# Attention with stride masks, a rotating token mixer and a gated mixture of attention experts: q loaded as diagonal blocks, float64 weights rebuilt in three bit operations and in halves, masks of 128 rows, the values of a pair in a row

## The chip, the cores and the metric

The kernel runs on one core of a Trainium2 chip. The metric is the device time in microseconds, as the median of several runs. The core has a matrix engine (TensorE; PE in the profile, PEld for its weight loads), VectorE (DVE), ScalarE (ACT), GpSimd (POOL) and SyncE (SP), which here only issues transfers.

## The reference

Four batches of 576 positions go through three blocks. The first is attention over 8 heads of 64; the first four heads see a window of 32 positions, the last four see positions that are equal modulo 32. The second mixes tokens and channels. The third is a mixture of four attention experts with a gate.

```python
# block 1, per head: local or strided mask, both causal
scores = scale * q @ k.T                     # scale = 1/8
scores = where(mask, scores, -1e9)
attn   = exp(scores - max); attn /= sum + 1e-9
x      = attn @ v                            # joined heads: (4, 576, 512)
# block 2
theta  = x @ w_theta                         # 512 x 512
y      = w_tok_r @ (x * cos(theta)) + w_tok_i @ (x * sin(theta))   # 576 x 576 each
u      = x + y
x      = u + max(u @ w_ch, 0)                # 512 x 512
# block 3: per expert q, k, v, causal attention, wo; the best two by gate are summed
```

The weights of block 2 arrive as float64.

## The kernel before

Everything is held with channels on the partitions: `X[b]` is batch b as 4 chunks of 128 channels by 576 positions. A float32 product at good precision is made of three matmuls (`mm3`, lines 240 to 243): each operand is split into a high and a low part, and high*high, high*low and low*high are added up.

**Block 1** is `attn_pair(b, pair)`, one call for each pair of heads: pairs 0 and 1 are local, 2 and 3 strided, and each pair has three groups of three or four tiles. For a group, q of two heads (288 KB a pair; k has 304 or 288 KB, v 432 or 297) is copied into a block-diagonal tile `qdiag` with the scale (lines 169 to 172: GpSimd for batch 0, ScalarE after), so that one matmul scores both heads. A mask matmul (line 178: bfloat16, 64 rows of `mask_l` or `mask_s` against `twice`, two identities side by side) opens the sum in PSUM, the score matmuls (line 182, float32, one for each tile) add to it. The softmax follows in one of two forms (`per_tile`, lines 193 to 203): either ScalarE takes the exponential of each tile with its maximum as bias, or VectorE subtracts the maximum and ScalarE takes all tiles at once. GpSimd divides (line 206), PE turns the probabilities (line 209), ScalarE moves them to SBUF (line 212), and PE multiplies by v (line 218: 64 output columns, two heads side by side in `av`); the result is copied into `X[b]` (lines 223 and 226). Each group does this by itself.

**The float64 weights** come through `load64` (lines 121 to 136), one chunk of 128 rows at a time, staged in `X[3]` and `X[2]`. ScalarE takes the magnitude of the upper word (131). VectorE then clamps it (132), shifts and masks it (133), ors in the top bits of the lower word (134) and the sign with the top exponent bit (135). `split_w` makes the high part on ScalarE and the low part on GpSimd or VectorE. `wth` (w_theta) has 4 chunks of 512, `wtk` (both token matrices) 9 chunks of 576, `wch` 4 chunks of 512.

**Block 2** for batch b is `theta(b, h)` and `rotate(b, h)` for the halves h = 0, 1 of the channels, then `tokens(b, h)`; `channels(b)` runs one batch later. `theta` has five tiles of positions of 12 matmuls each, in two PSUM buffers; VectorE reduces each result to one turn (264, 265), ScalarE takes the magnitude (266) and later cosine and sine (271, 272). `rotate` turns X on PE (279), multiplies on VectorE (289), and splits on ScalarE or VectorE (299, 301) and GpSimd (302). `tokens` is two halves of the positions by two chunks of 128 channels, 27 matmuls each.

**The order.** A planner (the tile framework) decides when each instruction goes out: each engine has one queue in program order of the planner's simulated schedule, and earlier code has priority when several are ready. The code's order is: pairs (0,0) and (0,1), `wth`, pairs (0,2) and (0,3); then for each batch theta, rotate, tokens, with the pairs of the next batch put between as filler. In batch 0 the whole of `wtk` is loaded right behind `theta(0, 0)`, line 369, and pairs (1,0) and (1,1) stand ahead of `tokens(0, 0)`. SP issues all transfers in one queue, and an issue that waits for a free buffer holds those behind it. `theta(b, 0)` needs all four pairs of its batch.

Of the kernel before, what the change touches and what calls it, by code (L numbers as in the profile page):

```python
# [32 lines left out]
MASKED = -1.0e9  # L33
INV2PI = 1.0 / (2.0 * math.pi)
# [3 lines left out]

TINY64 = float(np.array([0x38000000], np.uint32).view(np.float32)[0])
# [3 lines left out]
def fused_kernel(ctx: ExitStack, tc: tile.TileContext, ql, kl, vl, qs, ks, vs, wth, wtk, wch, wqk, wvg, wo, out):  # L43
    nc = tc.nc

    def f(ap):
        return ap.bitcast(F32)
# [10 lines left out]
    def select(ap, pattern, base, cm):  # L58
        nc.gpsimd.affine_select(out=ap, in_=ap, pattern=pattern, compare_op=ALU.is_ge, fill=MASKED,
                                base=base, channel_multiplier=cm)  # L60


    mask_l = new_mask("mask_l", [64, 4, LK])
    select(mask_l[:, 1, :], [[1, LK]], -1, -1)
    select(mask_l[:, 1, :], [[-1, LK]], WPAD, 1)
    nc.vector.tensor_copy(mask_l[:, 0, :], mask_l[:, 1, :])
    nc.vector.tensor_copy(mask_l[:, 2:4, :], mask_l[:, 1:2, :].to_broadcast([64, 2, LK]))
    nc.vector.memset(mask_l[:, 0, :WPAD], MASKED)
# [11 lines left out]
    mask_s = new_mask("mask_s", [64, 5, RQ])  # L80
    select(mask_s[:, 0, :], [[-1, RQ]], 0, 1)
    select(mask_s[:, 0, :], [[BLK, 3], [0, BLK]], BLK - 1, -1)
    nc.vector.tensor_copy(mask_s[:, 1:5, :], mask_s[:, 0:1, :].to_broadcast([64, 4, RQ]))
    nc.vector.memset(mask_s[:, 4, 2 * BLK:], MASKED)
    mask_c = new_mask("mask_c", [128, 128])
    select(mask_c, [[-1, 128]], 0, 1)
# [9 lines left out]
    qd = pha.enter_context(tc.tile_pool(name="qd", bufs=1, side="right"))  # L96
    qdiag = [[qd.tile([128, n, 2 * rw], F32, name=f"qdiag{rw}_{i}") for i in range(m)]
             for n, rw, m in ((3, LQ, 3), (4, RQ, 2))]
    for t in qdiag[0] + qdiag[1]:
        nc.vector.memset(t, 0.0)  # L100

# [19 lines left out]
    def load64(dst, src, kt, n, scale=1.0):  # L121


        hi, lo = dst
        for c in range(kt):
            raw = X[3].bitcast(U32).rearrange("p (a c) s -> p a (c s)", a=2)[:, c % 2, :2 * n]
            raw = raw.rearrange("p (n t) -> p n t", t=2)
            st = X[2][:, c % 4, :n]
            nc.sync.dma_start(raw, src[:, c, :].bitcast(U32).rearrange("p (n t) -> p n t", t=2))
# [6 lines left out]
            split_w(hi[:, c, :], lo[:, c, :], st, scale, nc.vector if c % 3 == 1 else nc.gpsimd)  # L136
# [5 lines left out]
    def attn_pair(b, pair, ps1, ain, apl, deep, qbufs, kbufs=2):  # L142
        local = pair < 2
        pj = pair % 2
        groups, rw, kw = (LOCAL, LQ, LK) if local else (STRIDED, RQ, RQ)
        kn = S + WPAD if local else S
        qr = ain.tile([128, S], F32, tag="q", bufs=qbufs, name=f"q_{b}_{pair}")
        kt = ain.tile([128, S + WPAD], F32, tag="k", bufs=kbufs, name=f"k_{b}_{pair}")
        nc.sync.dma_start(qr, (ql if local else qs)[b, pj])
        nc.sync.dma_start(kt[:, :kn], (kl if local else ks)[b, pj])  # L150
        loads = []
        for g, (j0, j1) in enumerate(groups):
            vg = ain.tile([128, 4, 2, HD], F32, tag="v", name=f"v_{b}_{pair}_{g}")
            nc.sync.dma_start(vg[:kw, :j1 - j0], (vl if local else vs)[b, pj, :, j0:j1])
            loads.append(vg)
        xo = X[b][:, pair, :]
        for g, (j0, j1) in enumerate(groups):
            vg = loads[g]
            n = j1 - j0

            qg = qdiag[pair // 2][(3 * pair + g) % len(qdiag[pair // 2])]
            q0, q1 = rw * j0, min(rw * j1, S)
            for h in range(2):
                hs = slice(64 * h, 64 * h + 64)
                for a, z_, m in ((q0, q1, n),) if (q1 - q0) % rw == 0 else ((q0, q0 + 2 * rw, 2), (q0 + 2 * rw, q1, 1)):
                    i0 = (a - q0) // rw
                    dst = qg[hs, i0:i0 + m, rw * h:rw * h + (z_ - a) // m]
                    src = qr[hs, a:z_].rearrange("p (n q) -> p n q", n=m)
# [39 lines left out]
            for i in range(n):  # L208
                nc.tensor.transpose(tp[:kw, i * rm:(i + 1) * rm], p[:rm, i * kw:(i + 1) * kw], ident[:rm, :rm])  # L209
# [3 lines left out]
            pt = pt[:, :n * rm].rearrange("p (n h q) -> p n h q", n=n, h=2)  # L213
            av = ps1.tile([128, 512], F32, tag="av", bufs=2, name=f"av_{b}_{pair}_{g}")
            for i in range(n):
                w = kw if local else wd[i]
                for h in range(2):
                    nc.tensor.matmul(av[64 * h:64 * h + 64, i * rw:i * rw + wd[i]], vg[:w, i, h, :],  # L218
                                     pt[:w, i, h, :wd[i]], start=True, stop=True)
            c = sum(wd)  # L220
            copy = nc.scalar.copy if b == 0 else nc.vector.tensor_copy
            if local:
                copy(xo[:, rw * j0:rw * j0 + c], av[:, :c])
            else:
                r0, nr = 3 * j0, c // BLK
                copy(xo.rearrange("p (t r) -> p r t", r=32)[:, r0:r0 + nr, :],
                     av[:, :c].rearrange("p (r t) -> p r t", t=BLK))
# [120 lines left out]
    with tc.tile_pool(name="ps0", bufs=2, space=PSUM) as ps0, tc.tile_pool(name="ain0", bufs=10) as ain0, \  # L348
            tc.tile_pool(name="apl0", bufs=6) as apl0:
        attn_pair(0, 0, ps0, ain0, apl0, 2, 4, 4)  # L350
        attn_pair(0, 1, ps0, ain0, apl0, 2, 4, 4)
        load64(wth_s, wth, 4, DM, INV2PI)
        for pair in range(2, 4):
            attn_pair(0, pair, ps0, ain0, apl0, 2, 4, 4)
# [7 lines left out]
    def next_pair(b, pair):  # L362
        if b + 1 < B:
            attn_pair(b + 1, pair, ps1, ain, apl, 1, 1)

    for b in range(B):
        theta(b, 0)
        if b == 0:
            load64(wtk_s, wtk, 9, S)
        else:  # L370
            next_pair(b, 0)
            channels(b - 1)
        rotate(b, 0)
# [19 lines left out]
        if b == 0:  # L393
            with tc.issue_after(sins[0, 1]):
                load64(wch_s, wch, 4, DM)
            next_pair(b, 2)
# [301 lines left out]
```

## Time and profile before

| | us |
|---|---|
| median of three runs | 602.59 |
| lowest, highest | 600.97, 603.19 |
| the profiled execution | 603.8 |
| its span on the core | 602.0 |
| PE busy | 571.9 (95%) |
| PE weight load busy | 525.3 (87%) |
| VectorE busy | 422.5 (70%) |
| ScalarE busy | 340.7 (57%) |
| GpSimd busy | 244.5 (41%) |

Matmuls are pipelined, so a PE that is busy all the time isn't one at its best pace: the step from one matmul's start to the next is the thing to read. The granted clock is a share of TensorE's 2.4 GHz. In the rows below, L182 is line 182 of the kernel; "x6" is the number of instructions in a row; what stands in square brackets is the idle time ahead of an instruction and what ended it.

### The profile page before, as it was taken

What the parts mean: (1) busy time and instruction counts of PE and PEld (TensorE: products, weight loads), DVE (VectorE), ACT (ScalarE), POOL (GpSimd) and SP (SyncE); (2) the same over time, 40 slices, a digit from 0 to 9 for tenths busy, and PEclk for the clock granted to TensorE, in tenths of its full rate; (3) what the DMA queues carried; (4) which work ended last, traced back from release to release, by engine and by line L of the source; (5) the groups of instructions that cost most, each with busy time, mean ns of one, the idle gap of its engine ahead of it and who ended that gap; (6) DMA issues with size and microseconds to landing.
All of it is one profiled execution on the core that took longest, in us unless ns stands there. A gap on an engine that the chain in (4) does not pass through costs nothing.

```text
span 602.0 us, 12582 instructions
## 1 busy us (share of the span) xinstructions
PE 571.9 (95%) x4560; PEld 525.3 (87%) x4560; DVE 422.5 (70%) x1209; ACT 340.7 (57%) x935; POOL 244.5 (41%) x336
## 2 busy tenths in 40 slices
PE   7985979899999999999999999999999999999997
PEld 5875859799999999989999999988989898989986
DVE  5689988794667646586545644289897878879881
ACT  4565796752655514646214532067577767857873
POOL 6763275441144411144300643345435624544452
PEclk9999878969999999999999999998999999999998
DMA  9723434121212111200010001100001000100112
GB/s 280 230 80 118 138 130 132 56 76 30 81 38 62 34 52 40 70 17 22 7 53 1 1 18 37 36 1 1 1 2 51 30 2 31 41 12 4 38 41 78
DMA packets 17365, 32.67 MB, mean 54 GB/s; under 512 B 2056, under 2 KB 9400, under 8 KB 17304
## 3 DMA queue, kind: packets, MB, share of 16 engines
q1 hardware_dynamic: 17304, 31.88, 17.3%
q8 instruction: 36, 0.59, 0.4%
q14 instruction: 25, 0.20, 0.1%
HBM read 27.15 MB, written 4.72 MB: 53 GB/s over the span
## 4 chain that ended last, share of the span: by engine, by line
PE 75%; DVE 12%; ACT 6%; issue 3%; DMA 2%; POOL 1%; POOLq 0%; DVEq 0%; ACTq 0%; SPq 0%
PE s L182 7%; PE y L241 6%; PE y L242 6%; PE y L243 6%; PE av L218 3%; PE tp L540 3%; PE tp L209 3%; PE g L241 3%; PE g L242 3%; PE g L243 3%; PE th L241 3%; PE th L242 2%; PE th L243 2%; PE o L564 2%; PE pq L241 2%
## 5 line engine op out<-in xcount | busy, mean ns | idle before, releaser
L241 PE MATMUL y<-wtk_hi,zhi 128*128 128x288 f32 x288 | 87.7, 305 | 0.4 <-DVE X L317 0.4
L242 PE MATMUL y<-wtk_lo,zhi 128*128 128x288 f32 x288 | 87.0, 302 | 0.0
L243 PE MATMUL y<-wtk_hi,zlo 128*128 128x288 f32 x288 | 86.2, 300 | 0.0
L302 POOL TENSOR_TENSOR zlo<-cs,zhi 128x512 fp32r<-128x512 f32 (+1 forms) x40 | 49.6, 1250 | 64.6 <-DVE zhi L299 40.2
L537 POOL TENSOR_SCALAR p<-p,sm,gt 128x256 f32<-128x256 f32 (+1 forms) x64 | 45.2, 709 | 58.8 <-DVE sm L535 44.7
L206 POOL TENSOR_TENSOR p<-p,sm 128x288 f32<-128x288 f32 (+2 forms) x48 | 33.1, 695 | 87.4 <-DVE sm L205 44.3
L530 ACT ACTIVATE p<-s,nm 128x128 f32<-128x128 f32 (+2 forms) x96 | 49.5, 517 | 14.8 <-DVE nm L519 10.0
L241 PE MATMUL th<-wth_hi,x_hi 128*128 128x256 f32 (+1 forms) x160 | 50.4, 316 | 7.2 <-DVE cs L265 6.7
L241 PEld LDWEIGHTS y<-wtk_hi,zhi 128*128 128x128 f32 x288 | 55.3, 192 | 0.7 <-DVE X L317 0.7
L242 PEld LDWEIGHTS y<-wtk_lo,zhi 128*128 128x128 f32 x288 | 55.3, 192 | 0.1
L243 PEld LDWEIGHTS y<-wtk_hi,zlo 128*128 128x128 f32 x288 | 55.2, 192 | 0.0
L237 POOL TENSOR_TENSOR x_lo<-X,x_hi 128x576 fp32r<-128x576 f32 x24 | 35.9, 1498 | 47.5 <-DVE x_hi L235 40.0
L182 PE MATMUL s<-k,qdiag 128*108 128x54 f32 (+2 forms) x320 | 54.3, 314 | 0.3 <-POOL qdiag L170 0.3
L182 PEld LDWEIGHTS s<-k,qdiag 128*108 128x108 f32 (+1 forms) x320 | 47.3, 222 | 6.5 <-issue 1.2
L519 DVE TENSOR_REDUCE nm<-s 128x1 f32<-128x128 f32 (+2 forms) x96 | 44.4, 469 | 5.4 <-PE s L517 4.1
L242 PE MATMUL th<-wth_lo,x_hi 128*128 128x256 f32 (+1 forms) x160 | 47.4, 297 | 0.0
L243 PE MATMUL th<-wth_hi,x_lo 128*128 128x256 f32 (+1 forms) x160 | 47.2, 296 | 0.0
L212 ACT COPY pt<-tp 96x384 f32<-96x384 f32 (+2 forms) x44 | 20.8, 473 | 39.6 <-PE tp L209 39.5
L241 PE MATMUL pq<-x_hi,wqk_hi 128*128 128x288 f32 x128 | 39.9, 312 | 0.7 <-DVE q L486 0.7
L549 DVE TENSOR_TENSOR ptlo<-tp,pthi 128x128 fp32r<-128x128 f32 (+4 forms) x80 | 38.1, 479 | 2.5 <-ACT pthi L548 1.9
L241 PE MATMUL g<-u_hi,wch_hi 128*128 128x288 f32 x128 | 39.3, 307 | 0.0
L241 PEld LDWEIGHTS th<-wth_hi,x_hi 128*128 128x128 f32 (+1 forms) x160 | 31.2, 195 | 8.6 <-DVE cs L265 7.6
(159 smaller groups left out, 1801.9 us busy)
## 6 DMA issues: line engine op xcount, KB each, us to landing
X<-in_wtk SPq DMA_DIRECT2D x9, 576.0 KB
out_t<-X SPq DMA_DIRECT2D x32, 144.0 KB
v<-in_vl SPq DMA_DIRECT2D x24, 144.0 KB
k<-in_kl SPq DMA_DIRECT2D x8, 304.0 KB
q<-in_ql SPq DMA_DIRECT2D x8, 288.0 KB
q<-in_qs SPq DMA_DIRECT2D x8, 288.0 KB
k<-in_ks SPq DMA_DIRECT2D x8, 288.0 KB
X<-in_wth SPq DMA_DIRECT2D x4, 512.0 KB
```

What stands on the lines that cost most here:

```text
L182: nc.tensor.matmul(s[:rm, i * kw:i * kw + w], qg[:, i, :], kt[:, k0:k0 + w], start=False, stop=i == n - 1)
L206: nc.gpsimd.tensor_tensor(tiles(p), tiles(p), each(sm), op=ALU.mult)
L212: copy(pt[:kw, :n * rm], tp[:kw, :n * rm])
L237: eng.tensor_tensor(lo, x, f(hi), op=ALU.subtract)
L241: nc.tensor.matmul(ps, ahi, bhi, start=first, stop=False)
L242: nc.tensor.matmul(ps, ahi, blo, start=False, stop=False)
L243: nc.tensor.matmul(ps, alo, bhi, start=False, stop=last)
L302: nc.gpsimd.tensor_tensor(lo, zf, f(hi), op=ALU.subtract)
L519: nc.vector.tensor_reduce(nm[:w, t + ci:t + ci + 1], s[:w, :c1 - c0], axis=AX.X, op=ALU.max, negate=True)
L530: nc.scalar.activation(p[:w, c0:c1], scs[ci][:w, :c1 - c0], AF.Exp, bias=nm[:w, t:t + 1], scale=1.0, accum_out=acc)
L537: eng.tensor_scalar(p[:w, :kn], p[:w, :kn], sm[:w, t:t + 1], gt[:w, t, e:e + 1], op0=ALU.mult, op1=ALU.mult)
L549: nc.vector.tensor_tensor(dst(ptlo), src, f(dst(pthi)), op=ALU.subtract)
```

## The change

- q comes from the host as diagonal blocks (`diag`), already in the form of `qdiag`, zeros included: a pair's q grows from 288 KB to 576 KB (local) or 594 KB (strided). `qdiag`, its memsets and the copies of lines 169 to 172 go. The scale goes into the exponential (`scale=SCALE`), and the masks are filled with -1e9 divided by it. In the form by tiles, ScalarE first scales the negated maximum, a tile of at most 128 by 4.
- `load64` loses the clamp of line 132: the magnitude is scaled by 2^-112 in the activation, and the masks of the bit operations take the whole exponent.
- `wtk` is loaded by halves of 288 columns: the first half of all nine chunks behind `rotate(0, 0)`, the second behind `rotate(0, 1)`; four staging places instead of two.
- The masks and `twice` have 128 rows, the lower 64 of the masks zero.
- Loads are a function of their own, `load_pair`. All four of batch 0 stand at the start, ahead of `wth`; that of pair (1,0) stands behind the first half of `wtk`.
- From batch 1 on, the value matmuls of a pair stand behind the pair's last transpose: groups 0 and 1 together into one `av` tile with one copy out, then group 2.
- The buffers of v fall from 10 to 9, those of the softmax from 6 to 5, in batch 0.

```diff
-    mask_l = new_mask("mask_l", [64, 4, LK])
+    mask_l = new_mask("mask_l", [128, 4, LK])
...
-        t = const.tile([64, 2, rw], BF16, name=f"twice{rw}")
-        nc.vector.tensor_copy(t, ident[:64, None, :rw].to_broadcast([64, 2, rw]))
+        t = const.tile([128, 2, rw], BF16, name=f"twice{rw}")
+        nc.vector.tensor_copy(t, ident[:, None, :rw].to_broadcast([128, 2, rw]))
...
-    def load64(dst, src, kt, n, scale=1.0):
+    def load64(dst, src, kt, n0, n1, scale=1.0):
...
+        n = n1 - n0
+        slots = S // n
...
-            nc.scalar.activation(st, f(up), AF.Abs)
-            nc.vector.tensor_scalar(st, st, TINY64, 1.0, op0=ALU.max, op1=ALU.mult)
-            nc.vector.tensor_scalar(w, w, 3, 0x3FFFFFF8, op0=ALU.logical_shift_left, op1=ALU.bitwise_and)
+            nc.scalar.activation(st, f(up), AF.Abs, scale=2.0 ** -112)
+            nc.vector.tensor_scalar(w, w, 3, 0x7FFFFFF8, op0=ALU.logical_shift_left, op1=ALU.bitwise_and)
             nc.vector.scalar_tensor_tensor(w, low, 29, w, op0=ALU.logical_shift_right, op1=ALU.bitwise_or)
-            nc.vector.scalar_tensor_tensor(w, up, 0xC0000000, w, op0=ALU.bitwise_and, op1=ALU.bitwise_or)
+            nc.vector.scalar_tensor_tensor(w, up, 0x80000000, w, op0=ALU.bitwise_and, op1=ALU.bitwise_or)
...
+    def load_pair(b, pair, ain, qbufs, kbufs):
...
+        qt = ain.tile([128, 11 * 2 * RQ], F32, tag="q", bufs=qbufs, name=f"q_{b}_{pair}")
...
-                    if b == 0:
-                        nc.gpsimd.tensor_scalar(dst, src, 1.0 / math.sqrt(HD), 1.0, op0=ALU.mult, op1=ALU.mult)
-                    else:
-                        nc.scalar.activation(dst, src, AF.Copy, scale=1.0 / math.sqrt(HD))
...
-                nc.tensor.matmul(s[:rm, i * kw:i * kw + w], qg[:, i, :], kt[:, k0:k0 + w], start=False, stop=i == n - 1)
+                nc.tensor.matmul(s[:rm, i * kw:i * kw + w], qt[:, j0 + i, :], kt[:, k0:k0 + w], start=False, stop=i == n - 1)
...
                 nc.vector.tensor_reduce(mx[:rm, :n], tiles(s), axis=AX.X, op=ALU.max, negate=True)
+                nc.scalar.activation(mx[:rm, :n], mx[:rm, :n], AF.Copy, scale=SCALE)
...
-                    nc.scalar.activation(p[:rm, :n * kw], p[:rm, :n * kw], AF.Exp)
+                    nc.scalar.activation(p[:rm, :n * kw], p[:rm, :n * kw], AF.Exp, scale=SCALE)
...
+            if b == 0 or g == 2:
+                for part in (done,) if b == 0 else (done[:2], done[2:]):
+                    values(b, pair, part, xo, turned)
+                done = []
+
+    def values(b, pair, part, xo, turned):
...
+        with tc.issue_after(turned.ins) if b else nullcontext():
+            for j0, pt, wd, vg in part:
...
+                        nc.tensor.matmul(av[64 * h:64 * h + 64, c0:c0 + wi], vg[:w, i, h, :], pt[:w, i, h, :wi],
+                                         start=True, stop=True)
...
         theta(b, 0)
-        if b == 0:
-            load64(wtk_s, wtk, 9, S)
-        else:
+        if b > 0:
             next_pair(b, 0)
             channels(b - 1)
         rotate(b, 0)
         if b > 0:
             next_pair(b, 1)
+        else:
+            load64(wtk_s, wtk, 9, 0, HALF)
+            load_pair(1, 0, ain, 2, 2)
         theta(b, 1)
         if b > 0:
             next_pair(b, 2)
         rotate(b, 1)
+        if b == 0:
+            load64(wtk_s, wtk, 9, HALF, S)
```

## Rows read from the trace of the kernel before

**Rows 1.** Windows by stage: PE, PEld, DVE, ACT, POOL busy us; clock; DMA.

```profile
0.00:47.30 47.30, 40.69 (x293) 32.92 (x293) 31.84 (x88) 27.59 (x99) 31.46 (x59) 1.00 0.65 192
47.30:99.40 52.10, 42.19 (x301) 36.36 (x302) 47.66 (x102) 36.14 (x94) 22.07 (x20) 0.80 0.42 135
99.40:115.00 15.60, 15.10 (x114) 14.63 (x112) 9.45 (x20) 11.67 (x32) 6.75 (x7) 1.00 0.17 54
115.00:145.20 30.20, 28.09 (x239) 25.79 (x240) 23.23 (x46) 12.34 (x24) 12.41 (x10) 0.83 0.22 66
145.20:388.00 242.80, 240.87 (x2068) 229.22 (x2068) 141.29 (x355) 106.69 (x250) 78.55 (x85) 1.00 0.12 36
```

**Rows 2.** Timeline of PE early in theta(0,0): start us, us, instruction.

```profile
48.73 0.42 PE L241 MATMUL th<-wth_hi,x_hi 128*128 128x256 f32 x1
48.94 0.42 PE L242 MATMUL th<-wth_lo,x_hi 128*128 128x256 f32 x1
```

**Rows 3.** Timeline, first stage: masks, scores, the last score, the first theta.

```profile
6.13 0.90 PE L178 MATMUL s<-mask_l,twice 64*128 64x288 bf16 x3
...
6.95 4.15 PE L182 MATMUL s<-k,qdiag 128*128 128x96 f32 x18
...
33.05 0.58 PE L182 MATMUL s<-k,qdiag 128*108 128x36 f32 x2
...
47.29 0.58 PE L241 MATMUL th<-wth_hi,x_hi 128*128 128x256 f32 x1 [0.50 <-ACT X L226]
```

**Rows 4.** The page: GB/s that DMA moved in 40 equal slices of the span.

```profile
GB/s 280 230 80 118 138 130 132 56 76 30 81 38 62 34 52 40 70 17 22 7 53 1 1 18 37 36 1 1 1 2 51 30 2 31 41 12 4 38 41 78
```

**Rows 5.** VectorE lines, 47.3 to 145.2: busy us, mean ns | idle before.

```profile
L134 DVE SCALAR_TENSOR_TENSOR X<-X,X 128x576 uint32<-128x576 uint32 x8 | 7.9, 990 | 0.1
L133 DVE TENSOR_SCALAR X<-X 128x576 uint32<-128x576 uint32 x8 | 6.6, 821 | 0.1
L135 DVE SCALAR_TENSOR_TENSOR X<-X,X 128x576 uint32<-128x576 uint32 x8 | 6.5, 814 | 0.1
...
L200 DVE TENSOR_TENSOR p<-s,mx 128x288 f32<-128x288 f32 x4 | 1.8, 443 | 0.0
```

**Rows 6.** Busy time of line 132 alone in that stage.

```profile
47.30:145.20 97.90, 5.36 (x11) 0.84 0.32 101
```

**Rows 7.** Timeline: a GpSimd subtraction and a VectorE bit operation side by side.

```profile
61.05 1.42 POOL L105 TENSOR_TENSOR wtk_lo<-X,wtk_hi 128x576 fp32r<-128x576 f32 x1 [4.07 <-ACT wtk_hi L103]
...
61.08 1.70 DVE L133 TENSOR_SCALAR X<-X 128x576 uint32<-128x576 uint32 x1
```

**Rows 8.** What PE waited for up to 140: us in total, times, longest.

```profile
PE th L241 <- DVE cs L265: 6.2, 2, 5.6
```

**Rows 9.** Timeline: the first token matmul, late in the second stage.

```profile
99.43 0.38 PE L241 MATMUL y<-wtk_hi,zhi 128*128 128x288 f32 x1
```

**Rows 10.** Timeline of PE at full pace: mask and scores; causal mask; values.

```profile
149.47 0.28 PE L242 MATMUL th<-wth_lo,x_hi 128*128 128x256 f32 x1
...
149.59 0.28 PE L243 MATMUL th<-wth_hi,x_lo 128*128 128x256 f32 x1
...
149.81 0.29 PE L178 MATMUL s<-mask_l,twice 64*128 64x288 bf16 x1
...
150.03 0.91 PE L182 MATMUL s<-k,qdiag 128*128 128x96 f32 x6
...
549.83 0.23 PE L517 MATMUL s<-mask_c,identb 128*128 128x128 bf16 x1
549.87 0.38 PE L241 MATMUL pq<-x_hi,wqk_hi 128*128 128x288 f32 x1
...
162.95 0.29 PE L243 MATMUL g<-u_hi,wch_lo 128*128 128x288 f32 x1
163.17 0.57 PE L218 MATMUL av<-pt,v 96*64 96x64 f32 x12
```

**Rows 11.** What the DMA queue of SP waited for: us, times, longest.

```profile
SPq L154 <- PE av L218: 101.1, 30, 7.7
```

More of the change, by code (lines that the diff above doesn't have):

```diff
@@ L33 @@
 MASKED = -1.0e9
+SCALE = 1.0 / math.sqrt(HD)
 INV2PI = 1.0 / (2.0 * math.pi)
@@ L37 @@
 TWO_PI = 6.283185
-TINY64 = float(np.array([0x38000000], np.uint32).view(np.float32)[0])
 @with_exitstack
@@ L95, in fused_kernel @@
     pha = ph1.enter_context(ExitStack())
[L96 to L100, printed above, removed]
     def split_w(hi, lo, st, scale=1.0, eng=nc.gpsimd):
@@ L145, in attn_pair @@
         groups, rw, kw = (LOCAL, LQ, LK) if local else (STRIDED, RQ, RQ)
+        nq = groups[-1][1]
+        qt = ain.tile([128, 11 * 2 * RQ], F32, tag="q", bufs=qbufs, name=f"q_{b}_{pair}")
+        qt = qt[:, :nq * 2 * rw].rearrange("p (n q) -> p n q", n=nq)
+        kt = ain.tile([128, S + WPAD], F32, tag="k", bufs=kbufs, name=f"k_{b}_{pair}")
         kn = S + WPAD if local else S
-        qr = ain.tile([128, S], F32, tag="q", bufs=qbufs, name=f"q_{b}_{pair}")
-        kt = ain.tile([128, S + WPAD], F32, tag="k", bufs=kbufs, name=f"k_{b}_{pair}")
-        nc.sync.dma_start(qr, (ql if local else qs)[b, pj])
+        nc.sync.dma_start(qt, (ql if local else qs)[b, pj])
         nc.sync.dma_start(kt[:, :kn], (kl if local else ks)[b, pj])
-        loads = []
+        vgs = []
         for g, (j0, j1) in enumerate(groups):
@@ L154, in attn_pair @@
             nc.sync.dma_start(vg[:kw, :j1 - j0], (vl if local else vs)[b, pj, :, j0:j1])
-            loads.append(vg)
+            vgs.append(vg)
+        loaded[b, pair] = qt, kt, vgs
+    def attn_pair(b, pair, ps1, apl, deep):
+        ps_of[b] = ps1
+        local = pair < 2
+        groups, rw, kw = (LOCAL, LQ, LK) if local else (STRIDED, RQ, RQ)
+        qt, kt, loads = loaded[b, pair]
         xo = X[b][:, pair, :]
+        done = []
         for g, (j0, j1) in enumerate(groups):
@@ L159, in attn_pair @@
             n = j1 - j0
[L161 to L168, printed above, removed]
-                    if b == 0:
-                        nc.gpsimd.tensor_scalar(dst, src, 1.0 / math.sqrt(HD), 1.0, op0=ALU.mult, op1=ALU.mult)
-                    else:
-                        nc.scalar.activation(dst, src, AF.Copy, scale=1.0 / math.sqrt(HD))
             wd = [min(rw, S - rw * j) for j in range(j0, j1)]
@@ L212, in attn_pair @@
             copy(pt[:kw, :n * rm], tp[:kw, :n * rm])
[L213 to L223, printed above, removed]
-            else:
-                r0, nr = 3 * j0, c // BLK
-                copy(xo.rearrange("p (t r) -> p r t", r=32)[:, r0:r0 + nr, :],
-                     av[:, :c].rearrange("p (r t) -> p r t", t=BLK))
+            done.append((j0, pt[:, :n * rm].rearrange("p (n h q) -> p n h q", n=n, h=2), wd, vg))
+            if b == 0 or g == 2:
+                for part in (done,) if b == 0 else (done[:2], done[2:]):
+                    values(b, pair, part, xo, turned)
+                done = []
+    def values(b, pair, part, xo, turned):
+        local = pair < 2
+        rw, kw = (LQ, LK) if local else (RQ, RQ)
+        r0 = part[0][0]
+        av = ps_of[b].tile([128, 512], F32, tag="av", bufs=2, name=f"av_{b}_{pair}_{r0}")
+        with tc.issue_after(turned.ins) if b else nullcontext():
+            for j0, pt, wd, vg in part:
+                for i, wi in enumerate(wd):
+                    w = kw if local else wi
+                    c0 = rw * (j0 - r0 + i)
+                    for h in range(2):
+                        nc.tensor.matmul(av[64 * h:64 * h + 64, c0:c0 + wi], vg[:w, i, h, :], pt[:w, i, h, :wi],
+                                         start=True, stop=True)
+        c = sum(sum(wd) for _, _, wd, _ in part)
+        copy = nc.scalar.copy if b == 0 else nc.vector.tensor_copy
+        if local:
+            copy(xo[:, rw * r0:rw * r0 + c], av[:, :c])
+        else:
+            copy(xo.rearrange("p (t r) -> p r t", r=32)[:, 3 * r0:3 * r0 + c // BLK, :],
+                 av[:, :c].rearrange("p (r t) -> p r t", t=BLK))
     def split_act(x, name):
@@ L347, in fused_kernel @@
     wch_s = wch_hi, wch_lo = new_split(wb, 4, DM, "wch")
[L348 to L352, printed above, removed]
+    with tc.tile_pool(name="ps0", bufs=2, space=PSUM) as ps0, tc.tile_pool(name="ain0", bufs=9) as ain0, \
+            tc.tile_pool(name="apl0", bufs=5) as apl0:
+        for pair in range(4):
+            load_pair(0, pair, ain0, 4, 4)
+        attn_pair(0, 0, ps0, apl0, 2)
+        attn_pair(0, 1, ps0, apl0, 2)
+        load64(wth_s, wth, 4, 0, DM, INV2PI)
         for pair in range(2, 4):
-            attn_pair(0, pair, ps0, ain0, apl0, 2, 4, 4)
+            attn_pair(0, pair, ps0, apl0, 2)
     zu = ph1.enter_context(tc.tile_pool(name="zu", bufs=4))
@@ L363, in next_pair @@
         if b + 1 < B:
-            attn_pair(b + 1, pair, ps1, ain, apl, 1, 1)
+            if (b + 1, pair) not in loaded:
+                load_pair(b + 1, pair, ain, 2, 2)
+            attn_pair(b + 1, pair, ps1, apl, 1)
     for b in range(B):
         theta(b, 0)
-        if b == 0:
-            load64(wtk_s, wtk, 9, S)
-        else:
+        if b > 0:
             next_pair(b, 0)
@@ L394, in fused_kernel @@
             with tc.issue_after(sins[0, 1]):
-                load64(wch_s, wch, 4, DM)
+                load64(wch_s, wch, 4, 0, DM)
             next_pair(b, 2)
@@ L659, in dmaj, with diag @@
         return a.transpose(0, 1, 3, 2).reshape(B, 2, 128, a.shape[2])
+    def diag(a, rw):
+        n = -(-a.shape[2] // rw)
+        o = np.zeros((B, 2, 2, HD, n, 2, rw), a.dtype)
+        for h in range(2):
+            for j in range(n):
+                w = min(rw, a.shape[2] - rw * j)
+                o[:, :, h, :, j, h, :w] = a[:, h::2, rw * j:rw * j + w].transpose(0, 1, 3, 2)
+        return o.reshape(B, 2, 128, n, 2 * rw)
     def vtiles(a, rw, kw):
```

46 lines of the change are left out of this document (24 added, 22 removed).

## The prediction

> **What bounds the kernel now.** I read the windows view first, cut where the work changes [rows 1]. From 145.2 to 388 PE is busy 240.9 of 242.8 us at full clock: there only fewer or shorter PE steps count. Ahead of that lie two stages in which it isn't so.
>
> The first, to 47.3, is block 1 of batch 0. PE is busy 40.7 us, yet it runs at the lower of its two clock levels (1.2 GHz): one theta matmul of 256 columns follows the other by 0.21 us [rows 2], and by 0.12 later [rows 10]. The windows view says 1.00 for this stage, and the pace contradicts it; I go by the pace. The last score ends near 33.6, and theta starts at 47.3 [rows 3]; the 14 us between are softmax steps of the last groups.
>
> The second, from 47.3 to 145.2, has theta, rotate and tokens of batch 0, and the attention of batch 1. VectorE is busy 47.7 of 52.1 us up to the first token matmul at 99.4 [rows 1, 9], while PE stands idle for 10 us and has a mean clock of 0.80. The waits view names the largest stop: theta waits once for 5.6 us for line 265 on VectorE, which stands behind bit operations on the weights [rows 8]. So in this stage VectorE comes last, and tokens start when `wtk` is through.
>
> **The first stage.** The diagonal q of pair (0,0) brings 288 KB more; at the 280 GB/s of the first slice [rows 4] that is 1.0 us until the first scores can start: +1.0 (0 to +2, should the next pair's loads be late too). GpSimd's copies go, but PE has no gap up to 33 that they could have made; nothing.
>
> The masks: at full clock the step into a 64-row mask is 0.22 us where 0.12 is usual (149.59 to 149.81), and the step from a mask of 288 columns to the first score is 0.22 too, where 0.12 x 288/256 = 0.13 is usual [rows 10]. That is 0.09 to 0.10 on each side, 0.20 a group. With 128 rows I take it to zero, by the nearest row: the causal mask of block 3 has 128 rows, is bfloat16 as well, and the next matmul follows by 0.04 us [rows 10]. At the lower level three masks in succession take 0.82 us to the first score [rows 3]; three steps of 0.24 would be 0.72, so 0.10 for one exit, the entry not seen: about 0.2 a group. Twelve groups, PE without a gap up to 33: -2.5 (0 to -3.4). The scaling of the maximum is one small ScalarE step more in each group, of which only the last lies on the path: +0.3. The tail of 14 us I leave as it is (-3 to +2): `wth` now comes behind all four pairs' loads, 2 x (576 + 304 + 432) + 2 x (594 + 288 + 297) KB = 5.1 MB, some 18 us at 280 GB/s, so its bit operations fall into the same place as before, and one of four goes. Sum -1.2, theta starts near 46.
>
> **The second stage**, 97.9 us. VectorE is busy 47.7 + 9.5 + 23.2 = 80.3 us [rows 1] and idle 17.6. Line 132 goes: -5.4 [rows 6]. The halves double the number of the other bit operations. The three take 7.9 + 6.6 + 6.5 = 21.0 us for 8 chunks [rows 5]. For a half the nearest row is line 200, 288 columns, 443 ns [rows 5]: 48 of them are 21.3 us. But the long ones are not long for their width alone: one shift, begun beside a GpSimd subtraction of 1.42 us, took 1.70 us [rows 7] against a mean of 0.82. If each half meets such a neighbour as often as a whole did, the excess is doubled; with 0.1 us of it in the mean (0.875) that is 48 x 0.1 = +5. I take +2 (0 to +5).
>
> On this the Trainium skill has a rule that speaks against halves: SBUF — State Buffer, "SBUF: two separate sides", says that VectorE and GpSimd share one port pair under an exclusive lock which the loser waits for in full. The pair of rows 7 looks like that. By the rule alone each half would wait as long as a whole, which is the upper end of +5 and would make the total 3 us later.
>
> So VectorE needs about 77 us here. PE needs: busy 85.4 us, of which at the lower level 2 x 0.20 x 52.1 + 2 x 0.17 x 30.2 = 31 us; if it is busy 27 of these, 13.5 are given back at full clock, and the switches of batch 1 give 3: about 69. Both are below 97.9, and what decides is how they overlap. Now everything that tokens need stands ahead of them: about 24 us of bit operations. Afterwards half of these stand behind `rotate(0, 1)`, beside the 14 us in which PE streams tokens (VectorE busy 9.5 of 15.6 there), theta's two steps come ahead of them in priority, and the softmaxes of pairs (1,0) and (1,1) follow both. I expect the first token matmul between 70 and 85 instead of 99.4, and the idle time of VectorE to fall from 17.6 to about 9: 77 + 9 = 86, **-12**. Bounds: the idle time stays, 94.5, -3.4; it falls to 3, 80, -18. What is next to come late is VectorE itself: the second half of `wtk`, `wch` and twelve softmaxes behind one another. ScalarE loses its q copies there; it is busy 36 of 52 us and comes last only for moments, so I count nothing.
>
> **From 145.2 to 388** attention of batches 2 and 3, 24 groups. Masks: 24 x 0.20 = -4.8. Values: the step into them is 0.22 against 0.13 (162.95 to 163.17) [rows 10], the way out taken as the same, 0.19 for each stretch. 24 stretches become two for each of 8 pairs: 8 x 0.19 = -1.5; if the two parts run together, 16 x 0.19 = -3.0. PE has no gaps that could swallow this. Sum **-6.3** (-2 to -8). Larger q loads change nothing: DMA has a share of 0.12. Batch 1's switches are in the second stage's sum. After 388 nothing is edited: 0, give or take 1.
>
> Sum against the profiled execution: 603.8 - 1.2 - 12 - 6.3 = 584.3. That run is 1.2 above the median, so **583** for the median.
>
> **The rivals.**
>
> *VectorE stays as idle as it is.* The order moves, but holes come elsewhere: tokens of the second positions wait for the second half of `wtk`, and PE has no filler because the softmaxes are behind it. For it: VectorE is nearly full up to 99.4. Then -3.4 in the stage: 603.8 - 1.2 - 3.4 - 6.3 - 1.2 = 592.
>
> *It packs well.* VectorE idle 3, values in one stretch, tail of the first stage shorter by 2: -1.2 - 2 - 18 - 7.8 = -29, 574. For it: PE and VectorE floors of 69 and 77.
>
> *The first stage goes to the high clock* once the masks no longer break PE's stream. Scores from 5.6 to 31 would take half, and the loads (18 us at 280 GB/s, plus 3) would end them near 22: 9 more, 574. Against it: PE is without a gap from 7 to 33 already, and the pace doesn't rise. The Trainium skill, TensorE: Matmul & The Clock Gate, "What's actually happening", has it that activity releases the throttle; by that rule alone the stage should have been fast before too, and here the trace doesn't bear it out.
>
> *The switch isn't in the rows* but in changing from bfloat16 to float32: the masks give nothing, 583 + 2.5 + 2.4 + 4.8 = 593. The 0.04 us of the causal mask speaks against it.
>
> *Slower: SP's queue stands at v.* There are three v buffers from batch 1 on, one pair's worth. Each was released group by group; now all three only when the pair's values have run. The queue of SP already waits 101 us in 30 places for value matmuls [rows 11], and behind a waiting v stands the next q, now twice as long: 432 + 594 KB, 3.7 us at 280 GB/s. Uncovered on five pairs of twelve it eats the gain; on seven, 583 + 26 = 609. Against it: in the long stretch a pair has some 27 us, and scores wait for q only, which is issued ahead of v.
>
> **How the numbers follow.** The forecast has 0.47 (578 to 588), VectorE idle as before 0.22 (588 to 597), packs well 0.14 (569 to 578), high clock 0.06, the switch elsewhere 0.05, SP's queue 0.06. The lower bounds together reach 571. All the upper ones together reach 601, which asks for five misfortunes at once; the idle time unchanged (592) with half of what the other upper ends add to it (5) gives 597. So 571 to 597, which leaves out SP's queue and the ends of two rivals. A measurement of this kernel tells about 0.5%, 3 us, from no change: faster than 599.6 has 0.90, within 0.04, slower 0.06.
>
> **What would show it.** First scores near 5.6; 0.12 us into a mask and out of it instead of 0.22; the first token matmul before 85, and VectorE's largest idle stretches gone; theta of batch 1 starting near 132 instead of 145; from there to the end of channels 6 us less; two stretches of value matmuls for each pair. The forecast is wrong if tokens start early and then stand still for the second half, if theta of batch 1 starts after 140, or if the bit operations of a half take over 0.65 us each.

## The result

| | before | after |
|---|---|---|
| median, us | 602.48 (600.97 to 603.19) | 581.33 (579.94 to 583.19) |
| the profiled execution, us | 603.8 | 579.94 |
| PE busy, us | 571.9 | 542.3 |
| VectorE busy, us | 422.5 | 412.3 |
| ScalarE busy, us | 340.7 | 316.2 |

Four runs each; the ratio is 0.9657, interval 0.9633 to 0.9680. The median is 1.7 us under the forecast of 583. But the stages differ from what I gave them. The windows view of after, cut at the first theta (37.7), the first token matmul (88.5), theta of batch 1 (132.3) and the first matmul of block 3 (362.1); columns as in rows 1:

```profile
0.00:37.70 37.70, 27.81 (x292) 23.45 (x292) 26.32 (x77) 25.16 (x102) 16.36 (x30) 0.86 0.62 210
37.70:88.50 50.80, 40.28 (x311) 37.05 (x312) 43.24 (x117) 32.90 (x102) 24.10 (x25) 0.77 0.65 200
88.50:132.30 43.80, 40.36 (x354) 38.19 (x354) 36.79 (x75) 21.83 (x48) 23.40 (x19) 0.96 0.28 92
132.30:362.10 229.80, 227.52 (x2025) 221.78 (x2023) 136.22 (x332) 89.60 (x196) 72.74 (x71) 1.00 0.14 43
362.10:578.20 216.10, 206.37 (x1584) 187.62 (x1584) 169.72 (x606) 146.72 (x438) 97.66 (x170) 1.00 0.08 26
```

The kernel before, cut at the same points of the work (its first stage stands in rows 1):

```profile
47.30:145.20 97.90, 85.38 (x652) 76.78 (x653) 80.34 (x166) 60.15 (x150) 41.22 (x35) 0.84 0.32 101
145.20:383.20 238.00, 236.55 (x2035) 225.08 (x2034) 140.21 (x351) 105.95 (x248) 74.18 (x74) 1.00 0.12 34
383.20:602.00 218.80, 209.30 (x1584) 190.53 (x1584) 170.08 (x606) 146.98 (x438) 97.65 (x170) 0.98 0.08 25
```

| stage | before | after | difference | predicted |
|---|---|---|---|---|
| first, to theta(0,0) | 47.3 | 37.7 | -9.6 | -1.2 |
| second, to theta(1,0) | 97.9 | 94.6 | -3.3 | -12 |
| to the end of channels | 238.0 | 229.8 | -8.2 | -6.3 |
| block 3 | 218.8 | 216.1 | -2.7 | 0 |
| sum | 602.0 | 578.2 | -23.8 | -19.5 |

In the first stage the matmuls run at both levels of the clock. The timeline of PE in after, scores of 96 columns and the end of the stage:

```profile
5.34 4.13 PE L180 MATMUL s<-k,q 128*128 128x96 f32 x18 [0.81 <-DMA k<-in_kl]
...
9.50 1.59 PE L180 MATMUL s<-k,q 128*128 128x96 f32 x12
...
20.33 0.70 PE L180 MATMUL s<-k,q 128*108 128x54 f32 x6
...
37.72 0.58 PE L253 MATMUL th<-wth_hi,x_hi 128*128 128x256 f32 x1 [0.84 <-ACT X L238]
```

The first 18 scores take 4.13 us, as in before [rows 3]; the next 12 take 1.59, so 0.13 each instead of 0.23. The clock's records in the trace say the same: full speed from 9.7 to 26.8. The last scores start at 20.33 instead of 33.05, and theta follows 17 us behind the last of them (37.7 less 20.8; 14 before). Theta itself starts at the low level, as in rows 2.

From 132 on the step from a mask to its score is 0.13 us, where rows 10 have 0.22, while the step into the values is still 0.20 (143.30 to 143.50), and the values of a pair stand in two stretches (24 and 12 matmuls):

```profile
134.05 0.29 PE L176 MATMUL s<-mask_l,twice 128*128 128x288 bf16 x1
134.18 0.80 PE L180 MATMUL s<-k,q 128*128 128x96 f32 x6
...
143.30 0.28 PE L255 MATMUL th<-wth_hi,x_lo 128*64 128x256 f32 x1
143.50 1.04 PE L231 MATMUL av<-pt,v 96*64 96x64 f32 x28
...
163.39 0.92 PE L231 MATMUL av<-pt,v 96*64 96x64 f32 x24
...
165.99 0.57 PE L231 MATMUL av<-pt,v 96*64 96x64 f32 x12
```

In the second stage VectorE's lines, 37.7 to 132.3 (busy us, mean ns | idle before), answer to rows 5 and 6:

```profile
L133 DVE SCALAR_TENSOR_TENSOR X<-X,X 128x288 uint32<-128x288 uint32 x17 | 8.7, 518 | 0.0
L132 DVE SCALAR_TENSOR_TENSOR X<-X,X 128x288 uint32<-128x288 uint32 x17 | 8.4, 492 | 0.1
L131 DVE TENSOR_SCALAR X<-X 128x288 uint32<-128x288 uint32 x16 | 7.1, 447 | 3.3 <-ACT X L130 3.3
L203 DVE TENSOR_SCALAR sm<-sm 108x4 f32<-108x4 f32 x4 | 4.3, 1082 | 0.0
```

VectorE is busy 80.0 us there, as before (80.3): the clamp is gone, and what came in its place is as long. And the wait for `wtk` is gone without tokens starting much earlier. The last low part of its first half, the end of `rotate(0,0)` and the first token matmul (GpSimd and PE, timeline):

```profile
67.52 0.79 POOL L100 TENSOR_TENSOR wtk_lo<-X,wtk_hi 128x288 fp32r<-128x288 f32 x1 [1.50 <-ACT wtk_hi L98]
...
81.36 0.72 POOL L314 TENSOR_TENSOR zlo<-cs,zhi 128x256 fp32r<-128x256 f32 x1 [0.54 <-ACT zhi L313]
...
88.50 0.38 PE L253 MATMUL y<-wtk_hi,zhi 128*128 128x288 f32 x1
```

What PE waited for between 37.7 and 132.3 (us, times, longest); the stop of rows 8 has shrunk to 0.8:

```profile
PE av L231 <- ACT pt L212: 3.2, 2, 3.0
...
PE y L254 <- POOL wtk_lo L100: 1.0, 1, 1.0
...
PE th L253 <- DVE cs L277: 0.8, 1, 0.8
```

One thing is needed to read the next section: the profiles of after with 64-row masks (598.82; six of its seven runs lie between 597.50 and 598.82 and one at 588.18), of before with q (606.72) and of before with q and masks (600.70) are of slow runs, so that the first kernel has no ratio in the table and the stages of the other two are left out.

### The profile page after: what moved, and what is told of

The parts are those of the page before. It is cut to its first block, busy times and chain, and to the rows that moved or that the text cites. A ratio compares the mean times of both kernels' runs of the same rounds, so it can differ in the third digit from the quotient of the medians.

```text
span 578.2 us, 12507 instructions
## 1 busy us (share of the span) xinstructions
PE 542.3 (94%) x4560; PEld 508.1 (88%) x4560; DVE 412.3 (71%) x1205; ACT 316.2 (55%) x882; POOL 234.3 (41%) x314
## 4 chain that ended last, share of the span: by engine, by line
PE 67%; DVE 14%; ACT 9%; DMA 5%; issue 2%; POOL 2%; SPq 0%; ACTq 0%; POOLq 0%; DVEq 0%
PE y L253 6%; PE y L254 6%; PE y L255 6%; PE tp L559 3%; PE th L253 3%; PE th L255 3%; PE th L254 3%; PE g L253 2%; PE g L254 2%; PE s L180 2%; PE g L255 2%; PE pq L253 2%; PE o L583 2%; PE s L533 2%; PE av L231 2%
## 5 line engine op out<-in xcount | busy, mean ns | idle before, releaser
L254 PE MATMUL y<-wtk_lo,zhi 128*128 128x288 f32 x288 | 85.6, 298 | 1.0 <-POOL wtk_lo L100 1.0
L255 PE MATMUL y<-wtk_hi,zlo 128*128 128x288 f32 x288 | 84.5, 296 | 0.0
L255 PEld LDWEIGHTS y<-wtk_hi,zlo 128*128 128x128 f32 x288 | 53.9, 188 | 0.0
L180 PEld LDWEIGHTS s<-k,q 128*108 128x108 f32 (+1 forms) x320 | 41.6, 201 | 6.0 <-issue 4.5
L180 PE MATMUL s<-k,q 128*108 128x54 f32 (+2 forms) x320 | 43.4, 279 | 3.4 <-DMA k<-in_kl 3.3
L212 ACT COPY pt<-tp 96x384 f32<-96x384 f32 (+2 forms) x44 | 20.8, 473 | 35.4 <-PE tp L208 35.2
L254 PE MATMUL pq<-x_lo,wqk_hi 128*128 128x288 f32 x128 | 37.9, 296 | 0.0
```

What stands on the lines that cost most here:

```text
L180: nc.tensor.matmul(s[:rm, i * kw:i * kw + w], qt[:, j0 + i, :], kt[:, k0:k0 + w], start=False, stop=i == n - 1)
L212: copy(pt[:kw, :n * rm], tp[:kw, :n * rm])
L254: nc.tensor.matmul(ps, ahi, blo, start=False, stop=False)
L255: nc.tensor.matmul(ps, alo, bhi, start=False, stop=last)
```

## The experiments

All stages in one table, from the profiled executions: to theta(0,0), then to theta(1,0), to block 3, to the end; the time is the median of the runs, the ratio is to the kernel before on the same chip.

| kernel | first | second | third | block 3 | us | ratio |
|---|---|---|---|---|---|---|
| before | 47.3 | 97.9 | 238.0 | 218.8 | 602.48 | 1 |
| after | 37.7 | 94.6 | 229.8 | 216.1 | 581.33 | 0.9657 (0.9633 to 0.9680) |
| after, masks of 64 rows | 45.1 | 98.7 | 234.7 | 218.5 | 598.06 | |
| before, masks of 128 rows | 48.4 | 92.0 | 234.1 | 217.4 | 594.61 | 0.9886 (0.9855 to 0.9917) |
| before, q from the host | | | | | 604.84 | 1.0046 (0.9995 to 1.0098) |
| before, both | | | | | 594.09 | 0.9909 (0.9878 to 0.9940) |
| before, both and the loads first | 37.5 | 96.9 | 232.0 | 217.4 | 585.63 | 0.9735 (0.9697 to 0.9772) |
| after, loads as before | 41.5 | 91.5 | 231.3 | 219.8 | 585.42 | 0.9745 (0.9706 to 0.9783) |
| after, wtk whole | 40.3 | 92.9 | 230.4 | 216.2 | 582.26 | 0.9690 (0.9658 to 0.9722) |
| after, values by group | 42.5 | 94.8 | 231.6 | 219.0 | 584.84 | 0.9725 (0.9683 to 0.9767) |
| after, one more operation a chunk | 37.8 | 102.9 | 229.6 | 217.4 | 589.68 | 0.9846 (0.9799 to 0.9893) |
| after, fewer transfers | 41.8 | 94.8 | 229.7 | 217.4 | 585.27 | 0.9732 (0.9692 to 0.9772) |
| after, idle matmuls | 38.2 | 97.1 | 229.7 | 217.5 | 584.93 | 0.9751 (0.9691 to 0.9812) |
| after, no 1e-9 | 37.3 | 93.1 | 228.4 | 217.4 | 578.94 | 0.9643 (0.9610 to 0.9677) |

### Masks

Theory 1: 64-row masks keep the clock down in the first stage. The rival: q and the loads let it rise. The edit on after (and its reverse, on before; `mask_s` and the copy into `twice` go with it):

```diff
-    mask_l = new_mask("mask_l", [128, 4, LK])
+    mask_l = new_mask("mask_l", [64, 4, LK])
...
-        t = const.tile([128, 2, rw], BF16, name=f"twice{rw}")
+        t = const.tile([64, 2, rw], BF16, name=f"twice{rw}")
```

> After, with masks and twice back at 64 rows; every engine's order of instructions is that of after. Theory 1, the 64-row masks hold the clock down in the first stage: PE stays at the lower level to theta, first theta near 47 instead of 37.7, and 24 later masks at 0.19 us give 4.6 more: 595 to 597. Theory 2, q from the host and the earlier loads let the clock rise: it rises near 10 us all the same, first theta near 40, total 588 to 589.

The time is 598.06. Every engine has its instructions in the order of after, so the rows of the masks are the only thing that differs in the program. Windows of the first stage, 16 to 20 us, after and then after with 64 rows:

```profile
16.00:20.00 4.00, 4.00 (x58) 3.88 (x57) 3.57 (x11) 2.33 (x8) 1.11 (x2) 1.00 0.71 265
```

```profile
16.00:20.00 4.00, 4.00 (x29) 3.52 (x28) 2.34 (x8) 1.56 (x8) 0.79 (x2) 1.00 0.74 295
```

PE is busy all the time in both, and does half as many matmuls in the second. The 1.00 there is no measurement: the clock's records begin at 30.1 us in that execution, with a rise. Theory 1 holds in this profile, with a little more than its number: 16.7 us by the medians; by the profiles 7.4 in the first stage, 4.1 in the second, 4.9 in the third and 2.4 in block 3 (on block 3, see below). Two things limit it. Some of the 7.4 can be chance, since a kernel with 128 rows and these same instructions also reached theta at 42.5 (last section). And the run at 588.18 is at theory 2's number; it has no profile. All 48 masks at 0.19 us would be 9.1 us by their steps alone (an estimate from rows 10), and that run is 6.9 us above after, so the clock may have risen early in it too. What stands is that the first rise came late in all three profiles with 64 rows and early in all eleven with 128 (last section).

> Before, with masks and twice of 128 rows and nothing else. Theory 1: the first stage goes to the high level between 10 and 15 us, first theta near 39 instead of 47.3, masks of batches 2 and 3 give 4.6: 589 to 590. Theory 2: the stage stays at the lower level, first theta near 44 (twelve groups at 0.26 us), 594 to 595.

594.61 is theory 2's number, but not its mechanism. The clock rises at 9.4 us, as theory 1 has it, and stays up for 6.8 us. The last score starts at 28.1 instead of 33.3, and yet theta starts at 48.4: what the scores gained, the 20.3 us behind them (14 before) gave back. So a high clock of this length is not sufficient, and theory 1 is half of the answer.

### q and the order of the loads

The q part of the change made on before alone, with the scale in the exponential:

```diff
-        nc.sync.dma_start(qr, (ql if local else qs)[b, pj])
+        nc.sync.dma_start(qt, (ql if local else qs)[b, pj])
...
-                        nc.gpsimd.tensor_scalar(dst, src, 1.0 / math.sqrt(HD), 1.0, op0=ALU.mult, op1=ALU.mult)
```

> Before, with q from the host as diagonal blocks and the scale in the exponential; masks of 64 rows, loads and weights as before. Masks of 128 rows alone left the first theta at 48.4 and gave the high clock for 7 us only. Theory 1a, both parts are needed (masks for the clock, q because GpSimd's copies, 12.8 of its 31.4 busy us, come next): the stage stays at the lower level, first theta near 45 as in after with 64-row masks, 597 to 600. Theory 2a, q alone makes the stage short: first theta near 40, 591 to 594.

604.84: no gain, 0.46% slower (interval from 0.05% faster to 0.98% slower). The median misses both theories; three of the ten runs (597.30 to 598.17) are where theory 1a has them, the other seven lie between 604.01 and 609.24, and why there are two groups stays open.

> Before, with 128-row masks and q from the host together. Theory 1a: first theta between 37.7 and 42.5, as in the three looks at after's first stage, and 594.6 less 8 is 584 to 588. Theory 3a, the order of the loads is needed too: first theta at 45 or later, 591 to 594.

594.09: no better than the masks alone, and what theory 3a gave. Next, the order of the loads by itself, taken back in after:

```diff
-        for pair in range(4):
-            load_pair(0, pair, ain0, 4, 4)
-        attn_pair(0, 0, ps0, apl0, 2)
-        attn_pair(0, 1, ps0, apl0, 2)
+        for pair in range(2):
+            load_pair(0, pair, ain0, 4, 4)
+            attn_pair(0, pair, ps0, apl0, 2)
```

> After, with the loads of batch 0 in the order of before: pairs 0 and 1, two chunks of wth (1 MB), then pairs 2 and 3. Theory 3a, the larger q needs this order, since the transfers set the first stage once PE is fast: first theta at 45 to 52 as in before with q alone (54.6) and with q and masks (52.3), 589 to 595. Rival, those two were late because their weights took more of VectorE: first theta 38 to 43, 580 to 584.

585.42, and theta at 41.5: here the rival is right on the stage, which lies among those of the other kernels made from after (37.3 to 42.5). Of the 5.9 us between the two profiled spans 3.7 are block 3, which isn't touched. The order that was taken out here, all four pairs ahead of `wth`, does more where it is added to before:

```diff
+        for pair in range(4):
+            loaded[0, pair] = load_pair(0, pair, ain0, 4, 4)
         attn_pair(0, 0, ps0, ain0, apl0, 2, 4, 4)
```

> Before, with 128-row masks, q from the host and the loads of all four pairs of batch 0 ahead of wth; weights, wtk's place, values and softmax buffers as before. Before with masks and q had its last score at 29.9 and the first theta at 52.3, 22.4 us behind it, where after needs 16.9 and before 14. If the order of the loads makes that difference once PE is fast: last score near 21, first theta 38 to 43, 584 to 588. If the tail behind the last score has another cause (the order of softmax steps and bit operations on VectorE and ScalarE): first theta 45 to 52, 588 to 594.

585.63, theta at 37.5, the last scores at 23.9. So with masks, q and loads together before has the first stage of after, and it is 4.3 us from after in time. The masks are needed (after with 64 rows: 45.1, and 598.06 in time), and in before the loads are. That q is needed, so that GpSimd's copies go (12.4 of its 31.5 us), is not shown: no run has masks and loads without it, and alone or with the masks it gained nothing. Why the order is worth 8.5 us in before and 4.1 in after, by the medians, I can't say from these runs: the planner makes another order of softmax steps and bit operations in each.

### The second stage

> After, with the whole of wtk loaded behind theta(0,0) as before, so nine chunks of 576 ahead of rotate. From theta(0,0) to theta(1,0) after needs 94.6 us where before needed 97.9, so little came of the halves or something else ate it. Theory 3, VectorE's sum sets this stage whatever its order: within 2 us of after, 580 to 583. Theory 4, the halves brought most of the 12 us I had put down and another part of the change lost them: 589 to 593.

```diff
-            load64(wtk_s, wtk, 9, 0, HALF)
...
-            load64(wtk_s, wtk, 9, HALF, S)
...
+            load64(wtk_s, wtk, 9, 0, S)
```

The line that is added stands behind `theta(0, 0)`. 582.26, second stage 92.9 against 94.6: the halves, my largest term, bring nothing. The first token matmul comes 47.1 us behind theta with the whole and 50.8 with halves.

> After, with one more VectorE operation for each chunk of the float64 weights (a maximum with a constant, which changes no value), 26 in all, where line 132 stood before. If VectorE's sum sets the second stage, as I had it: 22 operations of 0.3 us there, 6 to 7 us more, 587 to 588. If that stage is set by PE and its clock: 581 to 583.

```diff
+            nc.vector.tensor_scalar(st, st, TINY, 1.0, op0=ALU.max, op1=ALU.mult)
             nc.vector.tensor_scalar(w, w, 3, 0x7FFFFFF8, op0=ALU.logical_shift_left, op1=ALU.bitwise_and)
```

589.68, second stage 102.9, VectorE busy 90.6 instead of 80.0:

```profile
37.80:140.70 102.90, 84.22 (x666) 77.99 (x667) 90.55 (x219) 59.36 (x152) 43.21 (x44) 0.82 0.44 144
```

That is 8.3 us for 10.5 of VectorE, and speaks for VectorE as the bound. But the kernel with the loads as before speaks against it: VectorE is busy 11.2 us less there than in after, and the stage is only 3.1 us shorter:

```profile
41.50:133.00 91.50, 79.36 (x648) 74.00 (x649) 68.84 (x167) 51.01 (x138) 39.66 (x40) 0.85 0.42 138
```

The reverse was to show it once more:

```diff
-            nc.vector.tensor_scalar_add(sm[:rm, :n], sm[:rm, :n], 1e-9)
```

> After, without line 203, the 1e-9 on the sums of block 1, which changes no float32 sum of 1 or more. In the second stage its 14 instructions on 128 x 3 or 108 x 4 elements take 9.0 us of VectorE, some 1.1 to 1.4 us each beside a GpSimd operation. If VectorE's sum sets the stage at 0.8 us per us, as one more operation per chunk showed: 7 us less, 573 to 576. If the long ones are a wait that the next instruction takes over: 0 to 3 less, 578 to 581.

578.94, second stage 93.1. VectorE is busy 80.1 us, although 9.0 us of line 203 are gone. Its lines in that stage:

```profile
L133 DVE SCALAR_TENSOR_TENSOR X<-X,X 128x288 uint32<-128x288 uint32 x18 | 11.8, 666 | 0.0
L132 DVE SCALAR_TENSOR_TENSOR X<-X,X 128x288 uint32<-128x288 uint32 x18 | 9.7, 546 | 0.0
L131 DVE TENSOR_SCALAR X<-X 128x288 uint32<-128x288 uint32 x18 | 7.2, 414 | 0.3 <-ACT X L130 0.2
L131 DVE TENSOR_SCALAR X<-X 128x512 uint32<-128x512 uint32 x4 | 4.1, 1028 | 2.6 <-ACT X L130 2.6
```

The bit operations have grown: line 133 from 518 to 666 ns, line 131 on 512 columns from 419 to 1028. The second expectation holds in the time, and these lines fit it: the long time was a wait that others took over. At 578.94 this kernel has the lowest median of all, but its interval (0.9610 to 0.9677) overlaps that of after (0.9633 to 0.9680), so that it beats after isn't shown.

> After, with seven of the nine transfers of the second half of wtk left out (its bit operations run on what lies there, so half of the token weights are wrong): 2.0 MB less. DMA has a share of 0.79 from 37.7 to 65.8 where before had 0.43, and VectorE waits 5.7 us for the chunks. If the transfers hold VectorE up there: theta of batch 1 comes 3 to 6 us earlier, 575 to 578. If they are covered: 580 to 583.

```diff
+            if n0 == 0 or c < 2:
-            nc.sync.dma_start(raw, src[:, c, n0:n1].bitcast(U32).rearrange("p (n t) -> p n t", t=2))
+                nc.sync.dma_start(raw, src[:, c, n0:n1].bitcast(U32).rearrange("p (n t) -> p n t", t=2))
```

In the second half of `wtk` seven transfers are gone. Second stage 94.8: the transfers are covered there. The time of 585.27 missed both numbers, since theta started at 41.8 in this execution. Up to theta every engine has the instructions of after in the same order; what differs is the clock, which was up from 18.7 to 29.0 us here and from 9.7 to 26.8 in after.

### Idle matmuls, and values

> After, with six idle matmuls (identb times mask_l, 384 columns, into the tile that the transposes then overwrite) ahead of the transposes of the last five groups of batch 0, where PE stands waiting. If PE's idle time from 21 us on is what lets the clock fall at 26.8: it stays up or rises before theta, theta's first 24 matmuls take 0.12 instead of 0.21 us, 2.2 us, and theta starts no later: 577 to 580. If the 30 matmuls stand in the way of real ones, 30 x 0.16: 583 to 586.

```diff
+            if b == 0 and (pair == 3 or pair == 2 and g > 0):
+                for _ in range(6):
+                    nc.tensor.matmul(tp[:, :384], identb, mask_l.rearrange("p a c -> p (a c)"), start=True, stop=True)
```

584.93. The clock does stay up to 37.6 us, and theta starts at 38.2 all the same: from 21 us on PE waits for softmax steps, and a faster PE has nothing to hasten. Theta's first matmuls are at the low level again from 37.6 on.

> After, with the values of each group behind that group also from batch 1 on. At 0.19 us for a stretch and some 8 to 16 stretches more: 583 to 584. If all that the masks leave of the 8.2 us gained between theta(1,0) and the end of the channels, 3.6 us, came from the values: 585. If a long stretch only moves waits about: 580 to 582.

```diff
-            if b == 0 or g == 2:
-                for part in (done,) if b == 0 else (done[:2], done[2:]):
+            if True:
+                for part in (done,):
```

The third stage is 231.6 instead of 229.8: 1.8 us for 8 stretches, 0.22 each. The time is 584.84. The profiled execution (589.67) is longer than this median, for its first stage (42.5), whose code is that of after, and for block 3 (219.0).

## Why the prediction was right and its terms were not

**The total** came out at 581.3 for 583, with one term too large by 8.7 us and another too small by 8.4. A forecast whose terms fail in opposite directions was lucky in its total: two of its rivals, the high clock in the first stage and VectorE as idle as before, came true at once, and they cancel.

**The first stage** (-1.2, measured -9.6). The failing step is "Against it: PE is without a gap from 7 to 33 already, and the pace doesn't rise", by which the high clock got 0.06. I priced a mask at 0.2 us of its own, and gave the clock of everything around it nothing in the sum. PE's busy share did not tell the two apart: from 16 to 20 us it is 4.00 of 4.00 us with 64 rows and with 128. How a mask of 64 rows keeps the clock down is not shown. That it breaks the stream is the rival's idea, but the first 18 scores of before run 4.15 us with no mask between them [rows 3] and the clock doesn't rise, where those of after run 4.13 us and it rises at 9.7; and no run separates the longer steps from the 64 rows themselves. The small terms were right: scores at 5.34 (5.6 predicted), 0.13 us out of a mask. "GpSimd's copies go, but PE has no gap up to 33 that they could have made; nothing" held for q alone (604.84) and with the masks (594.09 beside 594.61). What the sum lacked is a term for the order of the loads: with all four pairs ahead of `wth`, masks and q brought theta to 37.5, where the masks alone left it at 48.4.

The steps around a 64-row mask were 0.22 us where 128 rows now have 0.13, and the step into the values is still 0.20. The Trainium skill, TensorEngine Tiling (Array Packing), "Key Properties", says that a change of the tiling mode drains the engine; the steps around the masks agree. For the values it stays open: they have 64 columns, but so has the theta matmul just ahead of them (128*64, at 143.30), and the step between the two is long all the same.

**The second stage** (-12, measured -3.3). This is the first rival, VectorE as idle as before, with its number (-3.4) and not its reason: PE waits only 1.0 us for the second half of `wtk` (y for wtk_lo). Two steps failed. First, "everything that tokens need": I took `wtk` for what tokens wait for, because it was through at 98.8 and tokens began at 99.4 [rows 9]. Its first half is now through at 68.3, and tokens still wait for `rotate(0,0)` (82.1), behind which PE first does what is left of theta(0,1). Second, "VectorE needs about 77": it is busy 80.0 and idle 14.6 (9 predicted). The 5.4 us of the clamp went, but the bit operations of the halves take 24.2 us for 50 where 21.0 for 24 stood (3.2 more; 2.3 predicted, 0.3 for the widths and 2 for the waits), and line 203 takes 9.0 where it took 6.8. Line 203 shows that a busy VectorE is in part a waiting one: taken out, its 9.0 us came back elsewhere. Adding work lengthened the stage, taking work or transfers away shortened it by 1.5 us at most. All kernels but the one with added work lie between 91.5 and 98.7 us here, and what sets this length is left open.

The bit operations of a half, 447 to 518 ns, are within what I gave them (under 650); the upper end, each half waiting as a whole does, wasn't reached.

**The third stage** (-6.3, measured -8.2). Masks 4.9 (predicted 4.8; 3.9 where only they change, in before), values 1.8 (1.5). The remaining 1.5 is near what q from the host and the loads give between two kernels (234.1 to 232.0). The sum had no term for ScalarE's q copies in this stage; that the 1.5 to 2 us are theirs isn't shown.

**Block 3** (0, measured -2.7) is not the change's. The trace of before has two spells of low clock there (416.3 to 419.7 and 590.4 to 593.8), after has none. Each such spell costs about 1.2: the six profiles with one of them take 217.4 or 217.5, the two with none (after, and after with wtk whole) 216.1 and 216.2, those with two, or one of twice the length, 218.5 to 219.0, and the one with a single and a double (after with loads as before) 219.8.

**SP's queue at v**: it waits 85.4 us in 22 places for value matmuls (101.1 in 30, rows 11), though the longest wait grew from 7.7 to 20.8; the slower case did not come.

## What to carry to other kernels

Where PE is busy all the time at the lower clock, look for matmuls of another shape in its stream, and price them by the clock of the whole stage and not by their own tenths of a microsecond; then look at once at who comes next, since the high clock alone didn't bring theta forward here (48.4), and did with q and the order of the loads (37.5). An operand that ends last before a consumer isn't the one it waits for until the others' ends have been read too. Busy time that is long for its size can be a wait, and a sum that subtracts it will promise too much.

## What the runs showed of the hardware

**The point at which the clock rises** is a matter of the execution. In the profiles of eleven kernels with 128-row masks it first rises between 9.3 and 18.7 us; in three with 64 rows it comes at 30.1, 51.1 and 60.8. After, after with values by group and after with fewer transfers have the same instructions in the same order up to theta. The clock is up from 9.7 to 26.8 us in the first, from 9.4 to 16.2 in the second and from 18.7 to 29.0 in the third, and theta starts at 37.7, 42.5 and 41.8. The window of the second from 16 to 20 us, beside the 58 matmuls of after:

```profile
16.00:20.00 4.00, 4.00 (x38) 3.32 (x38) 2.32 (x9) 1.93 (x6) 1.88 (x3) 0.52 0.83 325
```

So 4 to 5 us of a difference between two profiles of this kernel can be the clock's. The Trainium skill, TensorE: Matmul & The Clock Gate, "What's actually happening", has it that the monitor runs freely and doesn't start anew with a kernel; the spread of the rise agrees with that.

**A VectorE operation on four columns can take 1.4 us.** Line 203 takes 0.15 to 0.16 us by itself, and this beside GpSimd subtractions:

```profile
90.40 0.44 DVE L133 SCALAR_TENSOR_TENSOR X<-X,X 128x288 uint32<-128x288 uint32 x1
90.77 1.39 DVE L203 TENSOR_SCALAR sm<-sm 108x4 f32<-108x4 f32 x1
92.08 0.36 DVE L198 TENSOR_REDUCE mx<-s 108x4 f32<-108x216 f32 x1
92.37 1.15 DVE L203 TENSOR_SCALAR sm<-sm 108x3 f32<-108x3 f32 x1
```

```profile
89.55 2.58 POOL L249 TENSOR_TENSOR x_lo<-X,x_hi 128x576 fp32r<-128x576 f32 x1 [1.06 <-DVE x_hi L247]
...
92.10 1.40 POOL L249 TENSOR_TENSOR x_lo<-X,x_hi 128x576 fp32r<-128x576 f32 x1
```

The two operations of line 203 end at 92.16 and 93.52, the two subtractions at 92.13 and 93.50. In the second stage of after eight of the fourteen operations of line 203 take 0.4 to 1.4 us, and each of these ends within 0.04 us of the end of a GpSimd operation; the other six take 0.15 to 0.16. Line 133 took 0.44 beside the first subtraction, but that one took 2.58 us where the second took 1.40, so there the subtraction may have been the one that waited; elsewhere line 133 is long as well:

```profile
60.67 0.91 DVE L133 SCALAR_TENSOR_TENSOR X<-X,X 128x288 uint32<-128x288 uint32 x1
```

```profile
60.39 0.88 POOL L205 TENSOR_TENSOR p<-p,sm 128x288 f32<-128x288 f32 x1
```

The Trainium skill, SBUF — State Buffer, "SBUF: two separate sides", tells of an exclusive lock between the two engines whose loser waits in full; the ends of line 203 agree with that.
